# Softmax row sums by fewer products with ones, their additions shared by VectorE and GpSimd, and a magnitude taken on ScalarE

## The chip, the cores and the metric

The kernel runs on one core of a Trainium2 chip. The metric is the device time of one execution in microseconds (us); a time quoted as "the median" is that of three runs. One execution was also recorded instruction by instruction; all stretches and durations below come from that record.

The engines are called by the profile's names: PE is TensorE (PEld its weight loads), DVE is VectorE, ACT is ScalarE, POOL is GpSimd, SP is SyncE, which here issues the DMAs.

## What is computed

Three stages in a row: an attention whose queries are pooled in twos, a soft mixture of experts, and a two-layer network with a piecewise quadratic function between. Cut to what matters here:

```python
# attention: batch 4, heads 8, seq 1152, head_dim 64, all fp32
q_pool = q.reshape(B, H, S // 2, 2, D).mean(axis=3)          # 576 queries a head
scores = (1/np.sqrt(D)) * np.matmul(q_pool, k.transpose(0, 1, 3, 2))
scores = scores - np.max(scores, axis=-1, keepdims=True)
attn = np.exp(scores)
attn = attn / (np.sum(attn, axis=-1, keepdims=True) + 1e-09)   # the row sums
x = np.matmul(attn, v)                                       # -> [2304, 512] per token
x = moe(x, phi, w1, w2)                                      # 8 experts, 4 slots each
h = x @ w_in                                                 # w_in, w_out come as float64
g = where(h >= 1, h, where(h <= -1, 0, (h + 1)**2 / 4))
out = g @ w_out
```

`w_in` and `w_out` arrive as 64-bit floats, of which the kernel makes 32-bit floats itself with integer operations ("the conversion").

## The kernel before

**Attention.** Sixteen pairs of heads P = 0..15 follow each other. Of a pair, the 1152 keys are cut into nine blocks of 128; one block is a **step** g = 9P + c, and each step has two **half steps** (c, 0) and (c, 1), for the two heads. In half step (c, h) the program issues, in this order: `max_half` (L309 on PE, four pairs of matmuls into a PSUM tile `mx`, and L321 on DVE, the row maximum of that tile; this works for a pair that comes later, 11 steps ahead), `st` (L375 on PE, transposed scores of one key block for one head in a PSUM tile `st`; L380 on ACT, their exponential, 128 keys by 576 queries, into a tile `e` in SBUF), the row-sum products if any are due, `pv` (L410 on PE, exponentials times V of the step before, for one half of the queries), and then the half step's slot, a list of other work that a table fills. Every engine carries out its own instructions in the order of the program and waits by semaphores for the others. The PSUM tiles `mx` and `st` come from one pool of three buffers (`sc`), so that `st` of a half step needs the buffer that L321 of the half step before gave back.

**Row sums.** The sum over keys is taken by PE: matmuls with a column of ones (L397, `es_sum`) add the 128 partitions of a tile into spare columns of the accumulator `acc`. To have fewer of them, DVE first adds tiles `e` of the same head (L387, `es_add`). The table `GRP` says which key blocks are added together: blocks 0 and 1, 2 and 3, 4 and 5, while 6, 7 and 8 stay single: three additions a head, six a pair, in the slots (2, h), (4, h) and (6, h). The table `TAT` says where the products stand: after (3, 1) group 0, after (5, 1) group 1, after (7, 1) groups 2 and 3, after (9, 0), which is (0, 0) of the next pair, groups 4 and 5. One group is 8 matmuls of 32 columns of ones (2 stretches of queries by 4 quarters).

**Conversion.** 32 chunks of 128 by 512 are converted between the attention's steps by `cv_step(n, i)`, in 11 slots of a pair (`CVS`): (0,1), (1,0), (3,1), (4,0), (4,1), (5,0), (5,1), (6,0), (7,0), (8,0), (8,1). Step 0 is two DVE operations, L191 (magnitude: an "and" that clears the sign bit of the high word) and L192 (two bounds), step 1 is L194, step 2 L197, step 3 L200, after which the chunk is stored and chunk n + 2 is loaded (L180). For the first 16 chunks ACT then makes a rounded copy (L204) and a fifth slot holds L215 on DVE, their difference, and two stores (L217).

**Other work in slots** that a reader meets below: L264 on DVE, the low part of the keys in slots (1, 0) and (1, 1); L277 on POOL, the pooled queries, once per pair near (0, 0); L287 on DVE in (3, 0); L354 and L356 on DVE at (6, 1); the transposes of the finished pair on PE (L436 at (2, 0), L447 at (3, 0) and (3, 1), L474 at (4, 1)) with small DVE and ACT work.

After the attention come the experts (about 530 to 590 us of the profiled span) and the last two layers (L961 to L1038), which the change does not touch.

Of the kernel before, what the change touches and what calls it, by code (L numbers as in the profile page):

```python
# [8 lines left out]
F32 = mybir.dt.float32  # L9
# [3 lines left out]
AF = mybir.ActivationFunctionType  # L13
ALU = mybir.AluOpType
# [13 lines left out]
CV0 = 7  # L28
CVS = (0, 1), (1, 0), (3, 1), (4, 0), (4, 1), (5, 0), (5, 1), (6, 0), (7, 0), (8, 0), (8, 1)
# [6 lines left out]
WPH = 3  # L36
REA = 0

GRP = ((0, 1), (2, 3), (4, 5), (6,), (7,), (8,))
TAT = ((3, 1, (0,)), (5, 1, (1,)), (7, 1, (2, 3)), (9, 0, (4, 5)))  # L40


@with_exitstack
def fused_kernel(ctx: ExitStack, tc: tile.TileContext, q, k, v, phi, w1, w2, w_in, w_out, out):
    nc = tc.nc
# [8 lines left out]
    NP = B * H // 2  # L54
# [116 lines left out]
    cv = {}  # L171

    def cv_load(n):
        t = g2.tile([128, 512, 2], I32, tag="f64", bufs=2, name=f"f64_{n}")
        if n < 16:
            src = w_out[n * 128:(n + 1) * 128, :]
        else:
            dc, qr = divmod(n - 16, 4)
            src = w_in[dc * 128:(dc + 1) * 128, qr * 1024:(qr + 1) * 1024]
        nc.sync.dma_start(out=t, in_=src.rearrange("p (f t) -> p f t", t=2))  # L180
        cv[n] = t, None

    def cv_step(n, i):
        t, dst = cv[n]
        if dst is None:
            dst = g2.tile([128, 512], F32, tag="wst", bufs=2, name=f"wst{n}")
            cv[n] = t, dst
        d = dst.bitcast(I32)
        if i == 0:

            nc.vector.tensor_scalar(out=d, in0=t[:, :, 1], scalar1=0x7fffffff, scalar2=None, op0=ALU.bitwise_and)  # L191
            nc.vector.tensor_scalar(out=dst, in0=dst, scalar1=CLO, scalar2=CHI, op0=ALU.max, op1=ALU.min)  # L192
        elif i == 1:
            nc.vector.tensor_scalar(out=d, in0=d, scalar1=3, scalar2=0x3fffffff,  # L194
                                    op0=ALU.logical_shift_left, op1=ALU.bitwise_and)
        elif i == 2:
            nc.vector.scalar_tensor_tensor(out=d, in0=t[:, :, 1], scalar=-0x40000000, in1=d,  # L197
                                           op0=ALU.bitwise_and, op1=ALU.bitwise_or)
        else:
            nc.vector.scalar_tensor_tensor(out=d, in0=t[:, :, 0], scalar=29, in1=d,  # L200
                                           op0=ALU.logical_shift_right, op1=ALU.bitwise_or)
            if n < 16:
                hi = cvh[n] = g2.tile([128, DM], F32R, tag="whi", name=f"whi{n}")
                nc.scalar.activation(out=hi, in_=dst, func=AF.Copy)  # L204
            else:
                dc, qr = divmod(n - 16, 4)
                nc.sync.dma_start(out=wi_dr[dc][:, qr * 512:(qr + 1) * 512], in_=dst)
            if n + 2 < 32:
                cv_load(n + 2)

    cvh = {}

# [147 lines left out]
    E, Es, acc = {}, {}, {}  # L360
# [22 lines left out]
    def es_add(P, n, h, c):  # L383
        a, b = (E[P, GRP[n][0], h], E[P, c, h]) if c == GRP[n][1] else (Es[P, n, h], E[P, c, h])
        if c == GRP[n][1]:
            Es[P, n, h] = g3.tile([128, 2, HQ], F32, tag=f"es{h}", name=f"es{P}_{n}_{h}")
        nc.vector.tensor_tensor(out=Es[P, n, h], in0=a, in1=b, op=ALU.add)  # L387

    def es_sum(P, ns):
        for n in ns:
            for i, (c0, c1) in enumerate(((0, 192), (192, HQ))):
                for j in range(4):
                    h = j // 2
                    src = Es[P, n, h] if len(GRP[n]) > 1 else E[P, GRP[n][0], h]
                    nc.tensor.matmul(acc[P, i][32 * j:32 * j + 32, HQ:HQ + c1 - c0], lhsT=ones.to_broadcast([128, 32]),  # L397
# [191 lines left out]
    def at(g, slot, f, *a):  # L589
        sched.setdefault((g, slot), []).append((f, a))  # L590

    def plan(P):
        b = NK * P
        if P > 1:
            at(b - LQK, 0, load_qk, P)
            for h in range(2):
                at(b - 18, h, prep_khi, P, h)
                at(b - 17, h, prep_klo, P, h)
                at(b - 17, h, xpose_k, P, h)
            at(b - 18, 0, prep_qp, P)  # L600
            at(b - 16, 0, prep_qhi, P)
            at(b - 16, 0, xpose_q1, P)
            at(b - 15, 0, prep_qlo, P)
            at(b - 15, 1, dup_q1, P)
        if P > 0:
            at(b - 8, 1, load_v, P)
            at(b - 9 if P > 1 else 1, 1, s2_fill, P)
        for h in range(2):
            for n, cs in enumerate(GRP):
                for c in cs[1:]:  # L610
                    at(b + c + 1, h, es_add, P, n, h, c)
            at(b + 9, h, tail_raw, P, h)
            at(b + 9, h, tail_sum, P, h)
        for c, i, ns in TAT:
            pre[b + c, i] = P, ns
        last = P == NP - 1
        if not last:
            at(b + 11, REA, tail_rec, P)
        for i in range(2):
            at(b + (10 if last else 12), i if last else TXN[i], tail_xn, P, i)  # L620
            if last:
                at(b + 12, i, tail_mul, P, i)
        if not last:
            for c, sl, *a in TMUL:
                at(b + c, sl, tail_mul, P, *a)
        if last:
            at(b + 11, 0, tail_rec, P)
        at(b + 13, 1, tail_xt, P)
        if P % HPB == HPB - 1:
            q_ = P // HPB  # L630
            if last:
                at(b + LPT, 1, lg_part, q_)
                at(b + 11, 1, lg_half, q_)
                at(b + 14, 1, lg_sum, q_)
                at(b + 14, 1, warm, WARM[0])
                at(b + 14, 1, raw_mm, range(B - 1))
                at(b + 14, 1, warm, WARM[5])
                at(b + 15, 1, lg_max, q_)
                at(b + 15, 1, lg_exp, q_)
                at(b + 15, 1, lg_raw, q_)  # L640
                at(b + 16, 1, lg_nat, q_)
                at(b + 16, 1, warm, WARM[1])
                at(b + 18, 1, raw_mm, (B - 1,))
                at(b + 18, 1, warm, WARM[2])
                at(b + 17, 0, p_mm, q_)
                at(b + 17, 0, p_add, q_)
            else:
                for f, t in zip((lg_part, lg_sum, lg_max, lg_exp, lg_nat, p_mm, p_add), LGT):
                    at(b + t // 2, t % 2, f, q_)
# [9 lines left out]
    with tc.manual_schedule():  # L659
# [6 lines left out]
        for i in range(2):  # L666
            eng = nc.gpsimd if i else nc.vector
# [30 lines left out]
        at(5, 0, lambda: nc.sync.dma_start(out=phs, in_=phi.rearrange("(c p) s -> p c s", p=128)))  # L698
        for P in range(NP):
            plan(P)  # L700
        cvs = [(NK * P + c, sl) for P in range(NP - 1) for c, sl in
               CVS][CV0:]
        for n in range(32):
            for i in range(5 if n < 16 else 4):
                at(*cvs.pop(0), *((cv_step, n, i) if i < 4 else (cv_lo, n)))
        nsteps = NP * NK
        for g in range(-LEAD, nsteps + 1):
            mx = [divmod(g + LEAD, NK)] if not NK <= g + LEAD < 2 * NK else []
            mx += [(1, t) for t in range(NK) if P1G[t] == g]
            P, c = divmod(g, NK)  # L710
# [57 lines left out]
        n = 4 * NS + 4  # L768
# [353 lines left out]
```

## Time and profile before

| | |
|---|---|
| median of three runs | 808.16 us (807.66 to 808.5) |
| the profiled execution | 807.59 us |
| its span, first to last instruction | 805.4 us |
| PE busy / weight loads | 781.2 us (97%) / 562.7 us (70%) |
| DVE busy | 558.8 us (69%) |
| ACT busy | 434.0 us (54%) |
| POOL busy | 130.4 us (16%), nearly all of it after the attention |
| L397, products with ones | 768 matmuls in instructions of two passes: 1536 records |
| L387, additions for them | 96 on DVE |

How to read it: the profiled execution took 2.2 us more than its span, for what lies ahead of the first and behind the last instruction. Busy time of PE is modelled and overlaps from one matmul to the next, so a PE that waits for 0.2 us between two matmuls can still look busy; starts are what counts there. The shares are over the whole span, of which the attention is the first 530 us.

### The profile page before, as it was taken

What the parts mean: (1) busy time and instruction counts of PE and PEld (TensorE: products, weight loads), DVE (VectorE), ACT (ScalarE), POOL (GpSimd) and SP (SyncE); (2) the same over time, 40 slices, a digit from 0 to 9 for tenths busy, and PEclk for the clock granted to TensorE, in tenths of its full rate; (3) what the DMA queues carried; (4) which work ended last, traced back from release to release, by engine and by line L of the source; (5) the groups of instructions that cost most, each with busy time, mean ns of one, the idle gap of its engine ahead of it and who ended that gap; (6) DMA issues with size and microseconds to landing.
All of it is one profiled execution on the core that took longest, in us unless ns stands there. A gap on an engine that the chain in (4) does not pass through costs nothing.

```text
span 805.4 us, 19576 instructions
## 1 busy us (share of the span) xinstructions
PE 781.2 (97%) x8216; PEld 562.7 (70%) x8216; DVE 558.8 (69%) x879; ACT 434.0 (54%) x823; POOL 130.4 (16%) x104
## 2 busy tenths in 40 slices
PE   7899999999999999999999999999999999999998
PEld 6676766666766766667665676663478888888887
DVE  6878888787898787878977864225286777666620
ACT  4346556565665565565555645621276777565620
POOL 7000000000000000000000000000244445434330
PEclk8899999999999999999999999999999999999999
DMA  9777758897988778787897761869980000000000
GB/s 212 179 161 174 206 153 204 230 229 184 239 220 215 207 181 215 211 204 217 195 223 213 189 190 16 313 229 375 393 312 26 27 27 1 26 27 27 27 26 27
DMA packets 144103, 135.51 MB, mean 168 GB/s; under 512 B 80912, under 2 KB 100624, under 8 KB 143632
## 3 DMA queue, kind: packets, MB, share of 16 engines
q1 hardware_dynamic: 144016, 134.28, 60.6%
q8 instruction: 64, 1.05, 0.5%
q14 instruction: 23, 0.19, 0.1%
HBM read 91.29 MB, written 17.30 MB: 135 GB/s over the span
## 4 chain that ended last, share of the span: by engine, by line
PE 80%; DVE 9%; ACT 4%; DMA 4%; issue 2%; SPq 1%; ACTq 0%; DVEq 0%
PE st L375 16%; PE acc L410 14%; PE po L1025 8%; PE po L1024 8%; PE po L1026 8%; PE mx L309 7%; PE acc L397 7%; DVE mp L321 4%; ACT e L380 3%; PE h L961 2%; PE tx L447 2%; PE h L777 2%; DMA q<-qn 1%; PE s2o L829 1%; PE tb L474 1%
## 5 line engine op out<-in xcount | busy, mean ns | idle before, releaser
L380 ACT ACTIVATE e<-st 128x576 f32<-128x576 f32 x288 | 187.3, 652 | 162.3 <-PE st L375 156.6
L321 DVE TENSOR_REDUCE mp<-mx 128x1 f32<-128x576 f32 x282 | 211.2, 751 | 78.7 <-PE mx L309 77.9
L410 PE MATMUL acc<-e,vf 128*64 128x288 f32 x1152 | 195.3, 412 | 0.6 <-ACT e L380 0.6
L309 PE MATMUL mx<-K,q 128*64 128x288 f16 x1152 | 124.4, 296 | 8.6 <-DVE mp L321 5.4
L375 PE MATMUL st<-q,K 128*64 128x288 f16 x1152 | 121.9, 288 | 6.0 <-DVE mp L321 2.5
L375 PE MATMUL st<-q,S 128*64 128x288 f16 x1152 | 121.9, 286 | 0.4 <-DMA q<-qn 0.4
L309 PEld LDWEIGHTS <-q 128*64 128x64 f16 x1152 | 64.7, 111 | 68.7 <-issue 22.2
L974 DVE TENSOR_TENSOR r<-cl,r 128x1024 f32<-128x1024 f32 x34 | 81.2, 2388 | 38.6 <-ACT cl L973 38.6
L1025 PE MATMUL po<-wlo,ghi 128*128 128x512 f32 (+1 forms) x280 | 107.6, 384 | 0.0
L1024 PE MATMUL po<-whi,ghi 128*128 128x512 f32 (+1 forms) x280 | 107.6, 384 | 0.0
L1026 PE MATMUL po<-whi,glo 128*128 128x512 f32 (+1 forms) x280 | 107.2, 383 | 0.0
L980 POOL TENSOR_TENSOR glo<-r,ghi 128x1024 fp32r<-128x1024 f32 x34 | 81.7, 2403 | 101.6 <-ACT ghi L979 99.3
L375 PEld LDWEIGHTS <-K 128*64 128x64 f16 x1152 | 68.1, 109 | 28.4 <-issue 19.2
L277 POOL TENSOR_TENSOR qf<-qf 128x576 f32<-128x576 f32 x14 | 20.8, 1483 | 402.9 <-DMA qf<-in_q_dram 282.4
L410 PEld LDWEIGHTS acc<-e,vf 128*64 128x64 f32 x1152 | 75.9, 136 | 13.2 <-ACT e L380 1.8
L387 DVE TENSOR_TENSOR es<-e,e 128x576 f32<-128x576 f32 x96 | 70.7, 739 | 7.8 <-PE acc L397 7.8
L375 PEld LDWEIGHTS <-S 128*64 128x64 f16 x1152 | 69.8, 110 | 3.3 <-issue 0.6
L964 ACT ACTIVATE r<-h,cols 128x512 f32<-128x512 f32 x68 | 42.8, 685 | 32.8 <-PE h L961 31.3
L1026 PEld LDWEIGHTS po<-whi,glo 128*128 128x128 f32 x280 | 52.6, 188 | 10.5
L1024 PEld LDWEIGHTS po<-whi,ghi 128*128 128x128 f32 x280 | 52.7, 188 | 9.7
L1025 PEld LDWEIGHTS po<-wlo,ghi 128*128 128x128 f32 x280 | 52.7, 188 | 9.2
L965 DVE TENSOR_SCALAR cl<-h 128x512 f32<-128x512 f32 x68 | 43.7, 686 | 18.2 <-ACT r L964 16.7
(192 smaller groups left out, 838.2 us busy)
## 6 DMA issues: line engine op xcount, KB each, us to landing
w<-in_moe_w_dram SPq DMA_DIRECT2D x31, 1024.0 KB, 8.2
vf<-in_v_dram SPq DMA_DIRECT2D x16, 576.0 KB, 4.9
kf<-in_k_dram SPq DMA_DIRECT2D x30, 288.0 KB, 3.6
f<-in_moe_w_out_dram SPq DMA_DIRECT2D x16, 512.0 KB, 4.9
f<-in_moe_w_in_dram SPq DMA_DIRECT2D x16, 512.0 KB, 5.9
qf<-in_q_dram SPq DMA_DIRECT2D x30, 256.0 KB, 4.4
S<-K SPq DMA_DIRECT2D x16, 288.0 KB, 6.3
out_dram<-ob SPq DMA_DIRECT2D x17, 256.0 KB, 2.0
```

What stands on the lines that cost most here:

```text
L309: nc.tensor.matmul(ps[p0:p1, i, 0:HQ], lhsT=q1[P][:, t, p0:p1], rhs=kk[:, j * HQ:(j + 1) * HQ], start=True, stop=True)
L321: nc.vector.tensor_reduce(out=mp[P][:, t, a:a + 1], in_=ps[:, :, 0:HQ], op=ALU.max, axis=AX.XY)
L375: nc.tensor.matmul(ps[c0:c0 + 64, i, 0:HQ], lhsT=kk[:, ci, c0:c0 + 64], rhs=f[:, sl[i]], start=first, stop=not first)
L380: nc.scalar.activation(out=e, in_=ps[:, :, 0:HQ], func=AF.Exp, scale=ESC)
L387: nc.vector.tensor_tensor(out=Es[P, n, h], in0=a, in1=b, op=ALU.add)
L397: nc.tensor.matmul(acc[P, i][32 * j:32 * j + 32, HQ:HQ + c1 - c0], lhsT=ones.to_broadcast([128, 32]), rhs=src[:, j % 2, c0:c1], start=Fals ...
L410: nc.tensor.matmul(acc[P, i][h * 64:(h + 1) * 64, 0:HQ], lhsT=vt[P][:, h, c, :], rhs=E[P, c, h][:, i, :], start=False, stop=(c == NK - 1))
L974: nc.vector.tensor_tensor(out=r[:, sl], in0=cl[:, sl], in1=r[:, sl], op=ALU.add)
L980: nc.gpsimd.tensor_tensor(out=glo[n, qd][:, sl], in0=r[:, sl], in1=ghi[n, qd][:, sl].bitcast(F32), op=ALU.subtract)
L1024: nc.tensor.matmul(po, lhsT=ghi[n, qd][:, j, sl], rhs=whi[:, f, cs], start=(f == 0), stop=False)
L1025: nc.tensor.matmul(po, lhsT=ghi[n, qd][:, j, sl], rhs=wlo[:, f, cs], start=False, stop=False)
L1026: nc.tensor.matmul(po, lhsT=glo[n, qd][:, j, sl], rhs=whi[:, f, cs], start=False, stop=(f == 15))
```

## The change

- `GRP` becomes one group of seven blocks and two single ones. For each head blocks 0 to 6 are added into one tile, six additions in the slots (2, h) to (7, h), twelve a pair, each after the first in place on the running sum.
- `ESG` names the additions that POOL takes: those of blocks 2, 4 and 6 of head 1, in all pairs but the last: 3 of the 12. In the chain of head 1 the two engines take turns: DVE adds block 1, POOL 2, DVE 3, POOL 4, DVE 5, POOL 6. In the last pair DVE takes all twelve.
- `TAT` has one place, after (9, 0), where all three groups (seven blocks, block 7, block 8) are multiplied with ones: 24 matmuls a pair instead of 48.
- The magnitude (L191 on DVE) goes; in its place ACT writes the absolute value of the high word, read as a float, into the chunk's tile (`cv_abs`). It is issued one chunk ahead, in the slot where the chunk before makes its step 3.

```diff
-GRP = ((0, 1), (2, 3), (4, 5), (6,), (7,), (8,))
-TAT = ((3, 1, (0,)), (5, 1, (1,)), (7, 1, (2, 3)), (9, 0, (4, 5)))
+GRP = ((0, 1, 2, 3, 4, 5, 6), (7,), (8,))
+ESG = (2, 1), (4, 1), (6, 1)
+TAT = ((9, 0, (0, 1, 2)),)
...
+    def cv_abs(n):
+        t, dst = cv[n][0], g2.tile([128, 512], F32, tag="wst", bufs=2, name=f"wst{n}")
+        cv[n] = t, dst
+        nc.scalar.activation(out=dst, in_=t[:, :, 1].bitcast(F32), func=AF.Abs)
+
     def cv_step(n, i):
         t, dst = cv[n]
-        if dst is None:
-            dst = g2.tile([128, 512], F32, tag="wst", bufs=2, name=f"wst{n}")
-            cv[n] = t, dst
         d = dst.bitcast(I32)
         if i == 0:
 
-            nc.vector.tensor_scalar(out=d, in0=t[:, :, 1], scalar1=0x7fffffff, scalar2=None, op0=ALU.bitwise_and)
             nc.vector.tensor_scalar(out=dst, in0=dst, scalar1=CLO, scalar2=CHI, op0=ALU.max, op1=ALU.min)
...
             if n + 2 < 32:
                 cv_load(n + 2)
+            if n + 1 < 32:
+                cv_abs(n + 1)
...
-        nc.vector.tensor_tensor(out=Es[P, n, h], in0=a, in1=b, op=ALU.add)
+        eng = nc.gpsimd if P < NP - 1 and (c, h) in ESG else nc.vector
+        eng.tensor_tensor(out=Es[P, n, h], in0=a, in1=b, op=ALU.add)
...
+        at(CVS[CV0 - 1][0], 0, cv_abs, 0)
```

DVE before, in one pair while weights are converted, from half step (4, 0) on. In the names `mx_t_h` is the maximum's tile of block t, half h, `e_c_h` the exponentials of key block c, head h, `es_n_h` the sum of group n, head h, `wst` a chunk being converted:

```order
L321 TENSOR_REDUCE mp_3772<-mx_6_0_4119 128x1
L387 TENSOR_TENSOR es_1_0_4142<-e_2_0_4016,e_3_0_4068 128x576
L200 SCALAR_TENSOR_TENSOR wst_3946<-f_14_3670,wst_3946 128x512
L321 TENSOR_REDUCE mp_3772<-mx_6_1_4149 128x1
L387 TENSOR_TENSOR es_1_1_4176<-e_2_1_4047,e_3_1_4096 128x576
L215 TENSOR_TENSOR wst_3946<-wst_3946,whi_4145 128x512
L321 TENSOR_REDUCE mp_3772<-mx_7_0_4181 128x1
L191 TENSOR_SCALAR wst_4200<-f_15_3858 128x512
L192 TENSOR_SCALAR wst_4200<-wst_4200 128x512
L321 TENSOR_REDUCE mp_3772<-mx_7_1_4203 128x1
L194 TENSOR_SCALAR wst_4200<-wst_4200 128x512
L321 TENSOR_REDUCE mp_3772<-mx_8_0_4231 128x1
```

The same half steps on DVE after the change, where lines stand four to five lower in the file (L325 is L321 of before, L392 is L387, L202 is L200, L219 is L215, L194 is L192, L196 is L194):

```order
L325 TENSOR_REDUCE mp_3624<-mx_6_0_3959 128x1
L392 TENSOR_TENSOR es_0_0_3873<-es_0_0_3873,e_3_0_3914 128x576
L202 SCALAR_TENSOR_TENSOR wst_3698<-f_14_3530,wst_3698 128x512
L325 TENSOR_REDUCE mp_3624<-mx_6_1_3990 128x1
L392 TENSOR_TENSOR es_0_1_3897<-es_0_1_3897,e_3_1_3943 128x576
L219 TENSOR_TENSOR wst_3698<-wst_3698,whi_3984 128x512
L325 TENSOR_REDUCE mp_3624<-mx_7_0_4021 128x1
L392 TENSOR_TENSOR es_0_0_3873<-es_0_0_3873,e_4_0_3974 128x576
L194 TENSOR_SCALAR wst_3988<-wst_3988 128x512
L325 TENSOR_REDUCE mp_3624<-mx_7_1_4042 128x1
L196 TENSOR_SCALAR wst_3988<-wst_3988 128x512
L325 TENSOR_REDUCE mp_3624<-mx_8_0_4063 128x1
```

In (5, 0), the third reduction here, an addition of block 4 stands ahead of the conversion's step, and the magnitude is gone from it; the addition of block 4 of head 1 is on POOL, where it waits for the addition of block 3 just above.

PE before, at half step (0, 0), between the scores and the products with V; here `acc_0` and `acc_1` are the accumulator's two halves, `cols` the ones:

```order
L375 MATMUL st_0_0_1312<-q_2_1179,S_0_102 64x288
L397 MATMUL acc_0_883<-e_7_0_1212,cols 32x192 x2
L397 MATMUL acc_0_883<-e_7_1_1240,cols 32x192 x2
L397 MATMUL acc_1_911<-e_7_0_1212,cols 32x96 x2
L397 MATMUL acc_1_911<-e_7_1_1240,cols 32x96 x2
L397 MATMUL acc_0_883<-e_8_0_1275,cols 32x192 x2
L397 MATMUL acc_0_883<-e_8_1_1299,cols 32x192 x2
L397 MATMUL acc_1_911<-e_8_0_1275,cols 32x96 x2
L397 MATMUL acc_1_911<-e_8_1_1299,cols 32x96 x2
L410 MATMUL acc_0_883<-e_8_0_1275,vf_454 64x288
```

PE after the change at the same place (L379 is L375 of before, L402 is L397):

```order
L379 MATMUL st_0_0_1262<-q_2_1142,S_0_102 64x288
L402 MATMUL acc_0_863<-es_0_0_924,cols 32x192 x2
L402 MATMUL acc_0_863<-es_0_1_948,cols 32x192 x2
L402 MATMUL acc_1_889<-es_0_0_924,cols 32x96 x2
L402 MATMUL acc_1_889<-es_0_1_948,cols 32x96 x2
L402 MATMUL acc_0_863<-e_7_0_1174,cols 32x192 x2
L402 MATMUL acc_0_863<-e_7_1_1203,cols 32x192 x2
L402 MATMUL acc_1_889<-e_7_0_1174,cols 32x96 x2
L402 MATMUL acc_1_889<-e_7_1_1203,cols 32x96 x2
L402 MATMUL acc_0_863<-e_8_0_1223,cols 32x192 x2
```

The group of seven blocks has come in ahead of the two single ones, and at (3, 1), (5, 1) and (7, 1) no products with ones are left between scores and V.

## Rows read from the trace of the kernel before

**Rows 1.** The page: the chain that ended last, by engine.
```profile
PE 80%; DVE 9%; ACT 4%; DMA 4%; issue 2%; SPq 1%; ACTq 0%; DVEq 0%
```

**Rows 2.** Busy time by stretch: us, PE, PEld, DVE, ACT, POOL, PEclk, DMA, GB/s.
```profile
200.00:300.00 100.00, 98.54 (x1314) 68.78 (x1306) 84.57 (x145) 60.80 (x134) 4.69 (x3) 1.00 0.85 212
```

**Rows 3.** Groups by line and shape: busy us, mean ns | idle before <-releasers.
```profile
L321 DVE TENSOR_REDUCE mp<-mx 128x1 f32<-128x576 f32 x282 | 211.2, 751 | 78.7 <-PE mx L309 77.9
...
L204 ACT ACTIVATE whi<-wst 128x512 fp32r<-128x512 f32 x16 | 10.1, 631 | 6.7 <-DVE wst L200 4.7 <-DVE mm L354 1.8
```

**Rows 4.** Timeline of PE within one pair: start, us, instruction, merged.
```profile
268.21 0.44 PE L375 MATMUL st<-q,S 128*64 128x288 f16 x4
...
269.20 0.71 PE L410 MATMUL acc<-e,vf 128*64 128x288 f32 x4
...
277.57 0.41 PE L309 MATMUL mx<-K,q 128*64 128x288 f16 x4
...
278.06 0.41 PE L375 MATMUL st<-q,S 128*64 128x288 f16 x4
278.30 0.66 PE L410 MATMUL acc<-e,vf 128*64 128x288 f32 x4
278.79 0.41 PE L309 MATMUL mx<-K,q 128*64 128x288 f16 x4
...
279.28 0.41 PE L375 MATMUL st<-q,S 128*64 128x288 f16 x4
...
280.74 0.71 PE L410 MATMUL acc<-e,vf 128*64 128x288 f32 x4
281.28 0.41 PE L309 MATMUL mx<-K,q 128*64 128x288 f16 x4
```

**Rows 5.** Timeline of DVE in the same pair.
```profile
270.87 0.75 DVE L387 TENSOR_TENSOR es<-e,e 128x576 f32<-128x576 f32 x1
271.54 0.69 DVE L197 SCALAR_TENSOR_TENSOR wst<-f,wst 128x512 int32<-128x512 int32 x1
272.14 0.75 DVE L321 TENSOR_REDUCE mp<-mx 128x1 f32<-128x576 f32 x1
...
278.74 0.42 DVE L191 TENSOR_SCALAR wst<-f 128x512 int32<-128x512 int32 x1
279.20 0.43 DVE L192 TENSOR_SCALAR wst<-wst 128x512 f32<-128x512 f32 x1
279.54 0.75 DVE L321 TENSOR_REDUCE mp<-mx 128x1 f32<-128x576 f32 x1
```

**Rows 6.** Timeline of DVE, POOL and PE around one POOL addition.
```profile
349.02 0.75 DVE L321 TENSOR_REDUCE mp<-mx 128x1 f32<-128x576 f32 x1
...
349.44 1.41 POOL L277 TENSOR_TENSOR qf<-qf 128x576 f32<-128x576 f32 x1 [33.36 <-DMA qf<-in_q_dram]
...
349.69 1.78 DVE L264 SCALAR_TENSOR_TENSOR kn<-kf,kn 128x576 f16<-128x576 f32 x1
...
354.32 0.44 PE L309 MATMUL mx<-K,q 128*64 128x288 f16 x4 [0.80 <-DVE mp L321]
```

**Rows 7.** Timeline of PE: L309 at (4,0), (7,1), (3,0), (3,1), the next (4,0).
```profile
262.73 0.44 PE L309 MATMUL mx<-K,q 128*64 128x288 f16 x4
...
273.64 0.44 PE L309 MATMUL mx<-K,q 128*64 128x288 f16 x4
...
288.50 0.41 PE L309 MATMUL mx<-K,q 128*64 128x288 f16 x4
...
290.54 0.44 PE L309 MATMUL mx<-K,q 128*64 128x288 f16 x4
...
293.12 0.44 PE L309 MATMUL mx<-K,q 128*64 128x288 f16 x4
```

**Rows 8.** One line's instructions: ns min/median/max, first and last start in us.
```profile
L974 DVE TENSOR_TENSOR r<-cl,r x34: 1225/2421/2480, 596.8 to 771.5; 128x1024 f32<-128x1024 f32 x34
```

**Rows 9.** The conversion's first DVE line: ns min/median/max, first and last start.
```profile
L191 DVE TENSOR_SCALAR wst<-f x32: 404/418/1215, 51.0 to 460.6; 128x512 int32<-128x512 int32 x32
```

## The prediction

> **What bounds the kernel now.** I read the chain of waits first. PE carries 80% of it, DVE 9%, ACT 4% [rows 1]: the kernel is paced by PE, and where it isn't, mostly by DVE. The change touches the attention alone, so next comes a stretch from its middle [rows 2]: PE busy 98.5 of 100 us, DVE 84.6, ACT 60.8, POOL 4.7. DVE has some 15% left. The groups by line say where that room lies: DVE idles 78.7 us, nearly always because the next maximum has not come from PE [rows 3]. It is idle behind long PE work, not evenly, so the question must be asked half step by half step.
>
> The timeline of PE gives the price of a half step without extras: from one L309 to the next 278.79 − 277.57 = 1.22 us; from the scores to the products with V it needs 278.30 − 278.06 = 0.24 us [rows 4]. With one group of products with ones in between that gap is 269.20 − 268.21 = 0.99 us, with two 280.74 − 279.28 = 1.46 us [rows 4]. One group thus costs PE 0.75 us, two cost 1.22, and a further one in the same place about 0.5.
>
> The timeline of DVE, where it runs without gaps, gives the room that an operation takes from start to start: an addition 0.67 us (270.87 to 271.54), a conversion step with two tensors 0.60 (271.54 to 272.14), L191 0.46, L192 0.34 [rows 5], a reduction 0.67 (349.02 to 349.69) [rows 6]. A chunk of the first kind is L191 and L192, one like L192, and three of 0.60: 2.95 us over five slots, 0.59 a slot.
>
> Now one lap of a pair, between half steps (4, 0), (7, 1) and the next (4, 0) [rows 7], with (0, 1) in [rows 4]. **Stretch A**, (4, 0) to (7, 0), took 273.64 − 262.73 = 10.91 us. **B**, (7, 1) to (0, 0), 281.28 − 273.64 = 7.64. **C**, (0, 1) to (3, 1), 293.12 − 281.28 = 11.84. Together 30.4 us. In A PE needs 7 × 1.22 = 8.5 us, 0.75 for one group, and one set of transposes. DVE needs seven reductions (4.69), four additions (2.68) and six conversion slots (3.54): 10.91 us, just what A took. So A is already paced by DVE; the two short operations at (6, 1) come on top, and DVE ends about that late, some 0.4 us, into B. In B and C PE is the longer one and DVE idles.
>
> **The change part by part.** *Products with ones.* They leave (3, 1), (5, 1) and (7, 1) and grow by one group at (0, 0). PE saves 0.75, 0.75 and 1.22 and pays about 0.5: 2.2 us a pair, 35 us for 16 pairs if PE were the bound everywhere. It isn't: the 0.75 at (5, 1) lies in A, which DVE paces, and is worth nothing. B gains 1.22 − 0.5 = 0.7 us, C up to 0.75.
>
> *Additions on DVE.* Nine instead of six a pair, +2.0 us. A holds six of them instead of four, +1.34; C one more, in (3, 0).
>
> *Magnitude.* L191 leaves DVE: 0.46 less per chunk, so a conversion slot takes 0.50; A with its six slots saves 0.54 us. On ACT 32 new operations come in. The nearest row is ACT's copy of the same 128x512, 631 ns [rows 3]: 20 us in all, between 0 (ACT idles 39% of [rows 2]) and 20 us (each delays an exponential for which PE waits). I take 1 us, near the lower end, since ACT idles in most half steps. ACT waits there for the load and for the buffer of two chunks before; behind it the next exponentials are queued, and PE for them.
>
> *Additions on POOL.* 45 of them, three a pair. What one costs is in the trace. A POOL addition of 128x576 ran from 349.44 to 350.85. DVE's reduction out of PSUM, begun at 349.02, took its usual 0.75 us; but the next, L264, with two inputs in SBUF, began at 349.69 and took 1.78 us instead of some 0.75, to 351.47, which is 0.62 us after POOL's end. It did nothing while POOL ran. At 354.32 PE then waited 0.80 us for a maximum behind it [rows 6]. The same is seen on an addition, L974: 1225 ns at best, 2421 in the median, in the stage where POOL adds beside it [rows 8]. The additions L387 are of that kind, and so are the conversion steps with two tensors.
>
> When do the three start? Each waits for the DVE addition just ahead in the chain of head 1, in (2, 1), (4, 1), (6, 1), whose operand is then fresh; POOL is idle and starts at once. DVE goes on with what stands there (in (4, 1) a conversion step, which holds POOL up), then a reduction (0.67 us, not hindered), then an addition of head 0 in (3, 0), (5, 0), (7, 0). That one meets POOL with 1.41 − 0.67 = 0.75 us still to go. So DVE loses 0.75 us three times a pair, more than the 0.67 that the addition would have cost on DVE. Its bounds: 0 if DVE were idle there, 1.41 if POOL starts just ahead of it.
>
> *What the notes say of it.* The Trainium skill (Perfetto Trace Analysis, section Optimizing Scalar/DVE Operations) says that offloading from a saturated DVE to ScalarE or even GpSimd may make sense, and adds that a port shared by DVE and GpSimd may spoil the latter. By its first half the 45 additions would be free, which is the second case below; by the row above the second half decides.
>
> *The sum.* A: 4.69 + 6 × 0.67 + 6 × 0.50 = 11.7, two blocks of 0.75 make 13.2 us, +2.3. B: −0.7. C: in (3, 0) DVE has a reduction, the new addition, L287 (another 0.67) and a block, 2.75 us, where PE takes 290.54 − 288.50 = 2.0 [rows 7]; 0.4 of that may run over, 0.3 of the 0.75 is given back: −0.45. Together +1.15 us a pair. Conversion runs from 51 to 461 us [rows 9], 13.5 laps of 30.4: +15.5 us. In pair 14, where conversion is over, DVE has 3 us less in A, 10.2 us, about what PE's 9.3 and its transposes make there now: A −0.2, B −0.7, C −0.6, together −1.5. The last pair has no maxima to find and no POOL additions, so PE's full 2.2 us are gained. With 1 us for ACT: 15.5 − 1.5 − 2.2 + 1 = +12.8 us. The profiled execution of 807.6 becomes 820.4; the median of the three runs, 808.16, stands 0.6 above it, so I say 821 us.
>
> **The rivals.** *Second: the POOL additions cost DVE nothing* (they start where DVE idles or runs reductions, or POOL is the one that waits). Then A is 11.7, +0.8; B −0.7; C −0.75: −0.65 a pair, −9 us in 13.5 laps; pair 14 −2.0, the last −2.2, ACT +1: −12, 796 us; with another 0.4 of A run over into B, −17, 791. In general a lap changes by −0.65 + 2.4 × the block, and the total is below zero while the block is under some 0.35 us. For it: DVE's 78.7 us of idle time [rows 3]; against it: [rows 6, 8], and that in A, where two of the three fall, DVE has no idle time. The Trainium skill (SBUF — State Buffer, section Who interferes with whom) has it that issue order decides which of the two blocks; where DVE is first, POOL waits, which gives this second case.
>
> *Third: ACT becomes the bound as well.* The absolute value is asked for at the slot of step 3 of the chunk before; a load or a store that has not landed then holds up exponentials. If half of the 32 cost PE 0.63 us, 10 us more than no wait at all and 9 more than the sum has, 830; with POOL additions held back by DVE to the next gap (1.41 instead of 0.75 in one place a pair, +0.65 × 13.5 = 9) about 835. It decides once ACT is later than a half step leaves beside an operation of its own, 1.22 − 0.63, some 0.6 us.
>
> *Fourth: gains and losses cancel.* With a block of 0.30 to 0.40 us the laps cost 1.0 to 4.2 us, and the other terms give back 2.7: 806 to 810.
>
> **How the numbers follow.** Forecast (blocks as in the row, 812 to 828) 57%; third, above 828, 10%; fourth 8%; second, 788 to 806, 25%. The likeliest time is 821. For 8 in 10 the range must take in the upper part of the second case and most of the third: 795 to 834, which leaves out some 12% below and 5% above. A measurement of this kernel tells about 0.2%, 1.6 us, from no change. Faster by more than that: 0.27 (the second case and the fourth's edge); same: 0.06; slower: 0.67.
>
> **What would show it.** In the changed kernel's trace: additions of head 0 on DVE at (3, 0), (5, 0), (7, 0) lasting about 1.5 us instead of 0.75; stretch A near 13.2 us, B near 6.9, C near 11.4; PE waiting for L321's successor in A, where it now hardly does; DVE's share of a stretch near 90%; ACT's absolute values of about 0.63 us with hardly a wait ahead of exponentials. I am wrong if those additions last 0.75 us, if A is below 12 us, or if PE waits for ACT rather than DVE.

## The result

The changed kernel took 812.96 us in the median of five runs (811.26 to 814.66), 1.0064 times the kernel before, with a 95% interval of 1.0044 to 1.0085: some 5 us slower, where 13 us were forecast. The ratio is to four executions of the kernel before (806.72 to 808.5 us); a fifth took 1522 us and is left out. Run once more beside the experiments (the second measurement below) the changed kernel was at 815.23 us, 1.0089 (1.0073 to 1.0105). The profiled execution took 811.26 us, the fastest of the five; its span is 809.1 us, 3.7 us longer than before.

The page of the changed kernel, to be held against the table of before and [rows 3]:

```profile
PE 758.2 (94%) x7448; PEld 551.4 (68%) x7448; DVE 607.3 (75%) x898; ACT 451.3 (56%) x855; POOL 195.8 (24%) x149
...
L325 DVE TENSOR_REDUCE mp<-mx 128x1 f32<-128x576 f32 x282 | 209.1, 747 | 43.0 <-PE mx L313 42.1
...
L379 PE MATMUL st<-q,K 128*64 128x288 f16 x1152 | 126.2, 289 | 29.3 <-DVE mp L325 22.1
...
L392 POOL TENSOR_TENSOR es<-es,e 128x576 f32<-128x576 f32 x45 | 65.9, 1465 | 301.6 <-DVE es L392 271.3
...
L392 DVE TENSOR_TENSOR es<-es,e 128x576 f32<-128x576 f32 x115 | 116.0, 1011 | 3.7 <-ACT e L384 3.6
```

PE has lost 23 us of busy time with the 384 products, and DVE has won 48.5 us. The 115 additions that DVE makes in place take 1011 ns in the mean, where an addition by itself takes 746 (below, without POOL's): 115 × 0.265 = 30.5 us, 0.68 us for each of POOL's 45. PE now waits 22.1 us for DVE's maxima ahead of the scores; before it was 2.5:

```profile
L375 PE MATMUL st<-q,K 128*64 128x288 f16 x1152 | 121.9, 288 | 6.0 <-DVE mp L321 2.5
```

The same stretch as [rows 2], whose columns these are:

```profile
200.00:300.00 100.00, 91.76 (x1111) 64.38 (x1108) 91.04 (x142) 61.99 (x137) 18.92 (x13) 1.00 0.82 211
```

DVE is at 91 of 100 us instead of 85, PE at 92 instead of 98.5. The lap that [rows 7] cut into A, B and C, in the changed kernel: maxima's matmuls at (4, 0), (7, 1), (0, 1) and the next (4, 0), start and length in us.

```profile
266.55 0.44 PE L313 MATMUL mx<-K,q 128*64 128x288 f16 x4
...
278.50 0.44 PE L313 MATMUL mx<-K,q 128*64 128x288 f16 x4
...
288.21 0.41 PE L313 MATMUL mx<-K,q 128*64 128x288 f16 x4
...
299.28 0.44 PE L313 MATMUL mx<-K,q 128*64 128x288 f16 x4
```

A is 11.95 us (10.91 before), B 9.71 (7.64), C 11.07 (11.84). B, where the forecast had a gain of 0.7, has lost 2.1 in this lap. What happened on its way, DVE, POOL and PE in the order of time:

```profile
278.77 0.75 DVE L325 TENSOR_REDUCE mp<-mx 128x1 f32<-128x576 f32 x1
279.00 1.40 POOL L392 TENSOR_TENSOR es<-es,e 128x576 f32<-128x576 f32 x1 [5.78 <-ACT e L384]
...
279.43 1.58 DVE L392 TENSOR_TENSOR es<-es,e 128x576 f32<-128x576 f32 x1
...
280.94 0.68 DVE L202 SCALAR_TENSOR_TENSOR wst<-f,wst 128x512 int32<-128x512 int32 x1
281.54 1.41 DVE L325 TENSOR_REDUCE mp<-mx 128x1 f32<-128x576 f32 x2
...
282.34 0.44 PE L379 MATMUL st<-q,K 128*64 128x288 f16 x4 [1.93 <-DVE mp L325]
```

The reduction is not disturbed by POOL's addition. DVE's addition of head 0 in (7, 0) begins at 279.43, lasts until 0.6 us after POOL's end at 280.40, and takes 1.58 us; a conversion step and the reduction stand behind it, and PE, in (8, 0), waits 1.93 us. That is the block as foretold, but it is paid a half step later than A's end.

ACT's part is small here: 32 absolute values, and two short waits for a load (2.1 us together).

```profile
L187 ACT ACTIVATE wst<-f 128x512 f32<-128x512 f32 x32 | 21.6, 676 | 3.0 <-DMA f<-in_moe_w_in_dram 2.1 <-DVE kn L268 0.7
```

### The profile page after: what moved, and what is told of

It reads as the page before. It is cut to its first block, busy times and chain, and to the rows that moved or that the text cites. A ratio compares the mean times of both kernels' runs of the same rounds, so it can differ in the third digit from the quotient of the medians.

```text
span 809.1 us, 18313 instructions
## 1 busy us (share of the span) xinstructions
PE 758.2 (94%) x7448; PEld 551.4 (68%) x7448; DVE 607.3 (75%) x898; ACT 451.3 (56%) x855; POOL 195.8 (24%) x149
## 4 chain that ended last, share of the span: by engine, by line
PE 40%; DVE 10%; DMA 3%; issue 2%; ACT 1%; SPq 1%; DVEq 0%; ACTq 0%
PE po L1031 8%; PE po L1030 8%; PE po L1032 8%; DVE mp L325 4%; PE st L379 3%; PE acc L415 3%; DVE es L392 3%; PE h L967 2%; PE h L783 1%; PE s2o L835 1%; PE mx L313 1%; DMA whi<-wo_dr 1%; PE acc L402 1%; DMA w_last<-in_moe_w_dram 1%; SPq L909 1%
## 5 line engine op out<-in xcount | busy, mean ns | idle before, releaser
L325 DVE TENSOR_REDUCE mp<-mx 128x1 f32<-128x576 f32 x282 | 209.1, 747 | 43.0 <-PE mx L313 42.1
L415 PE MATMUL acc<-e,vf 128*64 128x288 f32 x1152 | 200.5, 409 | 0.3 <-ACT e L384 0.3
L379 PE MATMUL st<-q,K 128*64 128x288 f16 x1152 | 126.2, 289 | 29.3 <-DVE mp L325 22.1
L313 PE MATMUL mx<-K,q 128*64 128x288 f16 x1152 | 128.3, 294 | 12.8 <-DVE mp L325 8.5
L392 POOL TENSOR_TENSOR es<-es,e 128x576 f32<-128x576 f32 x45 | 65.9, 1465 | 301.6 <-DVE es L392 271.3
L379 PE MATMUL st<-q,S 128*64 128x288 f16 x1152 | 126.3, 287 | 0.0
L392 DVE TENSOR_TENSOR es<-es,e 128x576 f32<-128x576 f32 x115 | 116.0, 1011 | 3.7 <-ACT e L384 3.6
L313 PEld LDWEIGHTS <-q 128*64 128x64 f16 x1152 | 68.2, 110 | 72.4 <-issue 32.8
L379 PEld LDWEIGHTS <-K 128*64 128x64 f16 x1152 | 71.2, 109 | 60.6 <-issue 53.2
L415 PEld LDWEIGHTS acc<-e,vf 128*64 128x64 f32 x1152 | 83.1, 137 | 7.6 <-ACT e L384 3.5
L379 PEld LDWEIGHTS <-S 128*64 128x64 f16 x1152 | 73.1, 110 | 1.9
L1030 PEld LDWEIGHTS po<-whi,ghi 128*128 128x128 f32 x280 | 52.7, 188 | 9.6
L1031 PEld LDWEIGHTS po<-wlo,ghi 128*128 128x128 f32 x280 | 52.7, 188 | 9.3
```

The costliest lines, as they stand in the source:

```text
L313: nc.tensor.matmul(ps[p0:p1, i, 0:HQ], lhsT=q1[P][:, t, p0:p1], rhs=kk[:, j * HQ:(j + 1) * HQ], start=True, stop=True)
L325: nc.vector.tensor_reduce(out=mp[P][:, t, a:a + 1], in_=ps[:, :, 0:HQ], op=ALU.max, axis=AX.XY)
L379: nc.tensor.matmul(ps[c0:c0 + 64, i, 0:HQ], lhsT=kk[:, ci, c0:c0 + 64], rhs=f[:, sl[i]], start=first, stop=not first)
L392: eng.tensor_tensor(out=Es[P, n, h], in0=a, in1=b, op=ALU.add)
L415: nc.tensor.matmul(acc[P, i][h * 64:(h + 1) * 64, 0:HQ], lhsT=vt[P][:, h, c, :], rhs=E[P, c, h][:, i, :], start=False, stop=(c == NK - 1))
L1030: nc.tensor.matmul(po, lhsT=ghi[n, qd][:, j, sl], rhs=whi[:, f, cs], start=(f == 0), stop=False)
```

## The experiments

The theory was that of the forecast: a POOL addition stops DVE for about 0.68 us, and half steps that DVE paces pass that on to PE. The rival: POOL's additions are cheap, and DVE's nine instead of six, or the chain in which the engines take turns, or ScalarE, make the time. Every ratio is to the kernel before, run beside it on the same chip; runs from different chips are compared by their ratios.

**All twelve additions on DVE.**

```diff
-ESG = (2, 1), (4, 1), (6, 1)
+ESG = ()
```

> The changed kernel with all twelve additions a pair on DVE, none on POOL. Theory (a POOL addition stops DVE for about 0.68 us, so it saves DVE nothing against the 0.67 us that the addition takes there): the time stays where the changed kernel is, 811 to 815 us, and DVE's additions go back to 0.75 us each. Rival (POOL's additions are nearly free): 45 x 0.67 = 30 us more on DVE, of which some half comes through, 822 to 830 us.

Measured: 807.22 us, ratio 0.9978 (0.9961 to 0.9994). Below the theory's range, and on the other side from the rival's. DVE is nearly as busy as with POOL's help, 603.8 us against 607.3, and its additions are whole again:

```profile
PE 756.9 (94%) x7448; PEld 549.4 (68%) x7448; DVE 603.8 (75%) x943; ACT 451.2 (56%) x855; POOL 130.3 (16%) x104
...
L392 DVE TENSOR_TENSOR es<-es,e 128x576 f32<-128x576 f32 x160 | 118.8, 744 | 3.7 <-ACT e L384 3.6
```

So POOL's additions gave DVE nothing and cost the kernel 7 to 9 us (ratios 1.0064 and 1.0089 against 0.9978). With nearly equal time on DVE the difference probably lies in where it is spent. A likely reason, argued from the order and not measured by itself: an addition of 0.67 us on DVE stands in (3, 1), (5, 1) and (7, 1), half steps without another addition; the block of 0.75 us falls into (3, 0), (5, 0) and (7, 0), which hold an addition of head 0 already, and mostly a conversion step.

**Without POOL's additions** (three key blocks of head 1 are missing from the row sums of 15 pairs):

```diff
+        if P < NP - 1 and (c, h) in ESG:
+            return
```

> The changed kernel without the 45 additions on POOL, which are left out (three key blocks of head 1 are missing in the row sums of 15 pairs). Theory (they cost DVE 30 us, in the half steps that DVE paces): about the second case of the prediction, 793 to 800 us. Rival (POOL's additions cost nothing, DVE's own six or nine do): 810 to 814 us, as the changed kernel.

Measured: 795.72 us, ratio 0.9834 (0.9810 to 0.9857). This is the forecast's second case, 796 us, with the block at zero. DVE's rows:

```profile
L394 DVE TENSOR_TENSOR es<-es,e 128x576 f32<-128x576 f32 x115 | 85.6, 746 | 3.7 <-ACT e L384 3.6
```

The same 115 additions take 85.6 us instead of 116.0. And how long DVE still waits for PE's maxima, here, in the changed kernel and before (us in all, times, longest):

```profile
DVE mp L325 <- PE mx L313: 52.7, 49, 2.6
```
```profile
DVE mp L325 <- PE mx L313: 42.1, 36, 2.3
```
```profile
DVE mp L321 <- PE mx L309: 77.9, 76, 2.5
```

Of the 30.5 us by which POOL's additions stop DVE, 10.6 went into idle time that DVE had (52.7 − 42.1). The span grew by 809.1 − 791.8 = 17.3 us.

**The magnitude on ScalarE alone**, in the kernel before:

```diff
+        nc.scalar.activation(out=dst, in_=t[:, :, 1].bitcast(F32), func=AF.Abs)
...
-            nc.vector.tensor_scalar(out=d, in0=t[:, :, 1], scalar1=0x7fffffff, scalar2=None, op0=ALU.bitwise_and)
```

> The kernel before with the magnitude on ScalarE alone. Theory (DVE paces half steps (4,0) to (7,0), and gets back 0.46 us a chunk, 0.54 us a lap): 802 to 806 us. Rival one (DVE's load is not what paces that stretch): 808 us. Rival two (ScalarE is late with exponentials): 809 to 815 us.

Measured: 810.86 us, ratio 1.0017 (1.0005 to 1.0030). The theory's range is missed; both rivals hold in part. Stretch A of the lap that begins near 201 us, in the kernel before, and then here (PE at (4, 0) and (7, 1)):

```profile
201.32 0.44 PE L309 MATMUL mx<-K,q 128*64 128x288 f16 x4
...
211.88 0.44 PE L309 MATMUL mx<-K,q 128*64 128x288 f16 x4
```
```profile
204.11 0.44 PE L312 MATMUL mx<-K,q 128*64 128x288 f16 x4
...
214.68 0.44 PE L312 MATMUL mx<-K,q 128*64 128x288 f16 x4
```

10.56 and 10.57 us. DVE has half a us less to do in A, and A is not shorter: in this lap PE paced it. Nor is A shorter by more than 0.01 us in nine of the ten plain laps (those without the experts' logits, which some laps also compute). The lap that the forecast cut tells less: 10.91 us before, 11.22 here, with a wait of 0.48 us for an exponential in it. And this is what the magnitude costs on ACT, in (3, 1) and (4, 0) of a lap (start, length, instruction):

```profile
136.93 0.63 ACT L205 ACTIVATE whi<-wst 128x512 fp32r<-128x512 f32 x1
...
137.45 0.67 ACT L186 ACTIVATE wst<-f 128x512 f32<-128x512 f32 x1
...
138.01 0.65 ACT L383 ACTIVATE e<-st 128x576 f32<-128x576 f32 x1
...
138.71 0.44 PE L378 MATMUL st<-q,K 128*64 128x288 f16 x4 [0.97 <-ACT e L383]
```

The rounded copy and the absolute value stand ahead of the exponential, and PE waits 0.97 us for the buffer that it gives back. In all, PE waits 5.6 us for exponentials ahead of the scores, 0.7 before.

**The sums alone**, the changed kernel with the magnitude back on DVE (the diff above the other way round):

> The changed kernel with the magnitude back on DVE, that is the sums alone. Theory (DVE paces the middle of a lap, 32 x 0.46 = 15 us more on it, at least half comes through): 818 to 826 us. Rival (the magnitude is beside the path): 811 to 815 us.

Measured: 822.29 us, ratio 1.0157 (1.0139 to 1.0174), as the theory had it. The chain of waits by engine now has DVE on 37% of it (9% in [rows 1]):

```profile
PE 51%; DVE 37%; issue 5%; DMA 4%; ACT 2%; SPq 1%; DVEq 0%; ACTq 0%
```

By the ratios (1.0157 against 1.0064 and 1.0089) the magnitude on ScalarE is thus worth 5 to 8 us in the changed kernel, and costs 1 to 2 in the kernel before.

**POOL kept busy beside the kernel before**, with additions into a tile that nobody reads:

```diff
+    def busy(P, c):
+        if "busy" not in E:
+            E["busy"] = g1.tile([128, 2, HQ], F32, tag="busy", name="busy")
+        nc.gpsimd.tensor_tensor(out=E["busy"], in0=E[P, c, 1], in1=E[P, c, 1], op=ALU.add)
...
+            if h and P < NP - 2:
+                for c in (2, 4, 6):
+                    at(b + c + 1, h, busy, P, c)
```

> The kernel before, with 42 additions of 128x576 on POOL besides (three a pair in 14 pairs, at the places of the changed kernel's, into a tile that nobody reads). Theory (a POOL addition stops DVE by itself, for some 0.7 us, and the half steps around are full enough on DVE to pass half of it on): 818 to 826 us, with single DVE additions of about 1.5 us. Rival (what POOL costs in the changed kernel comes from the chain of head 1, in which the engines wait for each other): 807 to 810 us.

Measured: 818.07 us, ratio 1.0118 (1.0103 to 1.0134). At the theory's lower end and clear of the rival. DVE's work is the same as before, but its busy time is 587.1 us instead of 558.8: 28.3 / 42 = 0.67 us for each addition on POOL. They fall on other instructions than in the changed kernel: the single additions of 1.5 us that were expected are not seen, L387 is hardly longer (758 ns, 739 before). Among those that are longer are L200 (682 ns before) and L287 (776 before).

```profile
L387 DVE TENSOR_TENSOR es<-e,e 128x576 f32<-128x576 f32 x96 | 72.5, 758 | 7.8 <-PE acc L402 7.8
...
L200 DVE SCALAR_TENSOR_TENSOR wst<-f,wst 128x512 int32<-128x512 int32 x32 | 25.4, 794 | 0.0
...
L287 DVE SCALAR_TENSOR_TENSOR qn<-qf,qn 128x576 f16<-128x576 f32 x15 | 15.7, 1045 | 0.0
```

So the stop needs no chain between the engines. A third of it, 9.3 us, reaches the end here, where DVE has more room than in the changed kernel. No exponential in this trace waits for a tile that POOL still reads.

**All six additions of head 1 on POOL:**

```diff
-ESG = (2, 1), (4, 1), (6, 1)
+ESG = tuple((c, 1) for c in range(1, 7))
```

> The changed kernel with all six additions of head 1 on POOL in 15 pairs, 90 instead of 45, and six on DVE. Theory (each POOL addition takes from DVE at least what it saves, 0.68 against 0.67 us): not faster than the changed kernel, 810 to 820 us. Rival (POOL's additions are cheap, and what made the changed kernel slower is DVE's nine): 796 to 805 us.

Measured: 822.27 us, ratio 1.0185 (1.0163 to 1.0206), a little above the theory's range. DVE has 45 additions fewer and is busier, 610.4 us against 607.3:

```profile
PE 754.8 (92%) x7448; PEld 554.3 (67%) x7448; DVE 610.4 (74%) x853; ACT 450.6 (55%) x855; POOL 264.6 (32%) x194
...
L392 DVE TENSOR_TENSOR es<-es,e 128x576 f32<-128x576 f32 x85 | 85.9, 1012 | 3.7 <-ACT e L384 3.6
...
L202 DVE SCALAR_TENSOR_TENSOR wst<-f,wst 128x512 int32<-128x512 int32 x32 | 29.1, 910 | 0.0
```

**The changed kernel again**, beside that run:

> The changed kernel once more, on the same chip as the runs beside it. Both theories: 811 to 815 us, 0.6% above the kernel before.

Measured: 815.23 us, ratio 1.0089 (1.0073 to 1.0105), 0.2 us above the range.

**Fewer products where DVE has room.** If PE paces the kernel before, and DVE has room outside the half steps that the change filled, additions should go there. First groups of four, two, one, one and one: two more additions a pair, in (3, 0) and (3, 1), and no products after (3, 1); with the magnitude on ScalarE, and then without.

```diff
-GRP = ((0, 1), (2, 3), (4, 5), (6,), (7,), (8,))
-TAT = ((3, 1, (0,)), (5, 1, (1,)), (7, 1, (2, 3)), (9, 0, (4, 5)))
+GRP = ((0, 1, 2, 3), (4, 5), (6,), (7,), (8,))
+TAT = ((5, 1, (0,)), (7, 1, (1, 2)), (9, 0, (3, 4)))
```

> The kernel before with blocks 0 to 3 in one group (products after (5,1), none after (3,1)), 4 and 5 in another, all eight additions a pair on DVE, and the magnitude on ScalarE. Theory (the two more additions stand in (3,0) and (3,1), where PE has transposes and DVE has room, so PE's 0.75 us a lap come through): 10 us below the kernel that has the magnitude on ScalarE alone, 799 to 803 us. Rival (any further addition on DVE costs its 0.67 us): 809 to 813 us.

Measured: 806.06 us, ratio 0.9956 (0.9940 to 0.9971).

> The same groups of four, two, one, one and one, with the magnitude on DVE as before. Theory (the magnitude on ScalarE costs 1 to 2 us where DVE has room, and pays only where the additions fill DVE): 797 to 801 us, a little below the run with the magnitude on ScalarE. Rival (DVE needs the 0.46 us a chunk): above it, 803 to 808 us.

Measured: 803.60 us, ratio 0.9947 (0.9932 to 0.9961). They are 3.1 and 2.6 us above the upper ends of the theory's ranges. The second lies by its number in the rival's range, but not above the run with the magnitude on ScalarE, as the rival had it; the intervals of the two ratios overlap. Of the 12 us that PE saves (0.75 a pair), 4 to 5 came through.

Then blocks 6 and 7 together too, magnitude on DVE and on ScalarE:

```diff
+GRP = ((0, 1, 2, 3), (4, 5), (6, 7), (8,))
+TAT = ((5, 1, (0,)), (7, 1, (1,)), (9, 0, (2, 3)))
```

> Groups of four, two, two and one, magnitude on DVE: one more addition a head, in (8,0) and (8,1), one group of products less after (7,1). Theory (those half steps are short on PE, 1.22 us, and full on DVE with 1.93, but the long half step behind them takes up some 1 us): within 4 us of the run with groups of four, two, one, one, one, 797 to 804 us. Rival (PE paces everywhere): 8 us below it, 790 to 793 us.

Measured: 800.68 us, ratio 0.9902 (0.9888 to 0.9916), as the theory had it.

> Groups of four, two, two and one with the magnitude on ScalarE. Theory (the magnitude on ScalarE pays where DVE is filled by additions and costs where it has room; with ten additions a pair DVE is between the two): within 3 us of the same groups with the magnitude on DVE, 798 to 804 us. Rival (it is worth 9 us, as between the changed kernel with and without it): 790 to 793 us.

Measured: 805.08 us, ratio 0.9960 (0.9947 to 0.9973): 4.4 us above the same groups with the magnitude on DVE, and just outside the theory's range. With ten additions on DVE the magnitude on ScalarE costs more than with six (1 to 2 us) or eight (1 to 2.5), so how full DVE is does not alone decide where it is better placed.

Last, block 7 with 4 and 5, so that nothing stands after (7, 1):

```diff
+GRP = ((0, 1, 2, 3), (4, 5, 7), (6,), (8,))
+TAT = ((5, 1, (0,)), (9, 0, (2, 1, 3)))
```

> Groups of four (blocks 0 to 3) and three (4, 5 and 7), blocks 6 and 8 single, products after (5,1) and after (9,0), none after (7,1); magnitude on DVE. Theory (PE paces there, three groups in one place cost it some 0.25 us less than one and two): 2 to 4 us below groups of four, two, two and one, 796 to 800 us. Rival (the tiles of block 6 are held longer, and the exponentials that follow in them wait): 802 to 810 us.

Measured: 797.02 us, ratio 0.9867 (0.9850 to 0.9883), in the theory's range, 11 us below the kernel before and the best of the versions that compute everything. PE does 256 products fewer than before and waits less for maxima than in the changed kernel (6.7 us against 22.1 ahead of the scores):

```profile
PE 762.8 (96%) x7704; PEld 554.8 (70%) x7704; DVE 599.7 (75%) x943; ACT 433.9 (55%) x823; POOL 130.1 (16%) x104
...
L375 PE MATMUL st<-q,K 128*64 128x288 f16 x1152 | 123.2, 288 | 11.1 <-DVE mp L321 6.7 <-ACT xnr L463 0.7 <-ACT e L380 0.3
```

## Why the prediction was wrong

The direction and the mechanism held, the size did not: +13 us were forecast, +5 came, and +7 in the second measurement. Step by step:

- **The price of one block** was 0.75 us; it measured 0.68, from the longer additions, and 0.67 in the run that keeps POOL busy. Right.
- **The case without blocks** was put at 796 us and measured 795.7. The terms for the products, for nine additions on DVE and for the magnitude are right in their sum, which is in part luck: against the kernel before, the eight plain laps of the table below gained 2.4 us instead of 5.2 (in one of them the clock fell), the three with logits 4.4 instead of 2.0.
- **What a block is worth in time** is the step that failed, the term that was mis-sized. The sum let 1.8 of 2.25 us a lap through, 24.3 us in 13.5 laps. Measured, from the runs with and without the 45 additions, it is 17.3 us between the two profiled spans, 21.8 with the span of the second measurement (813.6), and 18.6 and 20.6 by the ratios (1.0064 and 1.0089, less 0.9834, of 808): 57 to 71% of 30.5 us where the sum had 80%. The rest went into idle time of DVE, of which the trace shows 10.6 us gone.
- **"A is already paced by DVE"** is the reading behind that, and it fell: without L191 A kept its 10.56 us in the lap shown with that run, which is the shortest A of the ten plain laps with and without L191. The sum of DVE's three kinds of work, 10.91 us, met the length of one lap's A by coincidence; only 0.35 us of that lap are above the shortest. Nor is it so that DVE has no idle time in A, which was held against the second rival; in the lap that the forecast cut, DVE waits there for PE, which has the products of (5, 1) to do:

```profile
270.19 0.76 DVE L321 TENSOR_REDUCE mp<-mx 128x1 f32<-128x576 f32 x1 [0.57 <-PE mx L309]
```

So DVE had some lead to lose in A before it paced anything.
- **One lap was taken for 13.5.** The lap that was cut into A, B and C went from 30.39 us to 32.73, more than forecast; the other plain laps of the table moved by −0.59 to +1.08. From the starts of L474 and L479, one for each pair, the spans differ from the one before like this, in the profile so far and in that of the second measurement (its slowest execution, 815.78 us, where the first profile was the fastest):

| stretch | forecast, us | measured, us | second, us |
|---|---|---|---|
| up to the first of these transposes (76 us before) | about +1.7 | −1.5 | 0.0 |
| eight plain laps | +9.2 | +5.0 | +6.9 |
| three laps that also do the experts' logits | +3.5 | −0.1 | +2.7 |
| one lap, in the first profile with a fall of the clock (below) | +1.2 | +4.3 | +2.6 |
| behind the conversion | −3.7 | −4.2 | −4.2 |
| all else (ACT; after the attention) | +1.0 | +0.2 | +0.2 |

In the second profile the clock fell in one of the laps with logits, which took 1.9 us more than before. The three laps with logits take 35.05 us before and 35.03 after in the mean. Without POOL's additions they win 4.4 us, so that a lap's blocks cost 1.5 us in them as well; what the forecast missed is that the rest of the change gains more there, 1.5 us a lap instead of 0.65. They were not looked at ahead of the result, though the trace of before shows them 4 us longer than the others.

- **Stretch by stretch**: B was to gain 0.7 us and lost 2.1 in the lap shown, because the block in (7, 0) is paid at (8, 0). A grew by less than 2.3 for the same reason: by 0.85 in the mean of nine plain laps, to 11.7 us, and by 1.04 in the lap shown, to 11.95. So one of the forecast's signs of being wrong, A below 12 us, came, while the signs of the block came too (additions of 1.57, 1.34 and 1.58 us at (3, 0), (5, 0) and (7, 0) of that lap, DVE at 91%, PE waiting for DVE). Taken together A and B grew by 1.46 us in the mean of these nine (the clock's lap left out, the one behind the conversion in), where 1.6 was forecast, and C shrank by 0.82 where 0.45 was forecast. The cut was wrong; the sum of a plain lap came to +0.64 where +1.15 was forecast.
- **ACT** was taken at 1 us. In the changed kernel its waits are small, as forecast; PE waits 3.7 us for exponentials ahead of the scores, 0.7 before. Alone, in the kernel before, the same step costs 1 to 2 us, by the third rival's mechanism.

The Trainium skill (SBUF — State Buffer, section Who interferes with whom) has it that a DVE instruction with two inputs in SBUF and a GpSimd instruction that reads SBUF shut each other out while they last, and that a reduction never meets this. The trace agrees with both: 1.58 us for the addition, 0.75 for the reduction under the same POOL instruction. It shows the other direction too: behind a conversion step with two tensors that had begun 0.22 us earlier, POOL's addition took 1.73 us instead of 1.40.

```profile
239.90 0.68 DVE L202 SCALAR_TENSOR_TENSOR wst<-f,wst 128x512 int32<-128x512 int32 x1
240.12 1.73 POOL L392 TENSOR_TENSOR es<-es,e 128x576 f32<-128x576 f32 x1 [5.70 <-DVE es L392]
```

The warning of the Trainium skill (Perfetto Trace Analysis, section Optimizing Scalar/DVE Operations) that moving work from DVE to GpSimd might not help is met here in its strict form: 45 additions moved left DVE 3.5 us busier.

What stays open: why the additions on POOL cost 7 to 9 us more than the same on DVE at nearly equal busy time of DVE. That the block's place is the reason was argued from the order of the instructions; no run moved the place alone. TensorE's clock is not the reason: granted, it is 0.991 to 0.992 in the mean over the runs of either kernel. Open as well is why the magnitude on ScalarE helps the changed kernel and hurts the others.

## What to carry to other kernels

Before work goes from VectorE to GpSimd, price it by what the neighbour loses: here an addition of 0.67 us on DVE became 1.4 us on POOL and 0.68 us of standstill on DVE. When an engine has 15% left, ask in which half steps: four more additions a pair, in (3, h) and (8, h) (groups of four and three), gave 11 us with the products that they save; six more, in (3, h), (5, h) and (7, h), gave 2 with the magnitude on ScalarE, though they save more products. And cut more than one lap before multiplying by thirteen, those with extra work above all.

## What the runs showed of the hardware that was not expected

**A wait, and a fall of the clock behind it.** In one lap of the changed kernel the granted clock fell. PE had waited 1.92 us for a maximum, until 117.7 us; behind it (stretch, length, busy PE, PEld, DVE, ACT, POOL, granted clock, DMA, GB/s):

```profile
117.72 0.44 PE L379 MATMUL st<-q,K 128*64 128x288 f16 x4 [1.92 <-DVE mp L325]
```
```profile
115.00:120.00 5.00, 3.07 (x30) 1.78 (x27) 3.93 (x5) 2.34 (x4) 0.79 (x1) 0.92 1.10 249
120.00:125.00 5.00, 5.00 (x74) 3.77 (x72) 1.85 (x3) 1.30 (x2) 1.40 (x1) 0.74 0.98 302
125.00:130.00 5.00, 5.00 (x66) 3.86 (x64) 4.14 (x7) 3.95 (x9) 0.00 (x0) 1.00 0.11 27
```

0.74 of full speed over 5 us means that about half of it ran at 1.2 instead of 2.4 GHz. The lap took 35.26 us, 4.3 more than before. Another lap has a wait of 1.93 us at the same half step (shown above) at a clock of 1.00 and took 2.3 us more than before. And in the profile of the second measurement the same lap has the same wait, with the clock at 1.00 behind it:

```profile
119.28 0.44 PE L379 MATMUL st<-q,K 128*64 128x288 f16 x4 [1.93 <-DVE mp L325]
```
```profile
120.00:125.00 5.00, 5.00 (x84) 3.57 (x84) 2.33 (x4) 2.28 (x4) 1.41 (x1) 1.00 1.01 245
```

There the lap took 2.6 us more than before. Of the 4.3 us some 1.7 are thus the clock's: a fall behind such a wait cost nearly the wait's length again, and the wait alone does not bring it about.

**An absolute value is hardly dearer than a copy, but comes at a place.** ACT took 676 ns for it, 631 for the copy of the same size [rows 3]; the cost that counted, in the kernel before, was the exponential behind it.
